# PSUM drains given to one engine each, a new issue order, and a last tile in two column halves

## The chip, the cores and the metric

The kernel runs on one core of a Trainium2 chip. The metric is the device time of one execution, in microseconds (us). "Span" is the time from the first to the last instruction in a profiled execution; in the runs here the measured time is 1.7 to 1.8 us longer. A transfer "lands" when its data has arrived; landing times are the issue time plus the time to landing. PSUM is the memory that matmuls write to, and from which ACT or DVE "drain" the result. The TensorE clock of the runs was 0.98 to 1.0. Runs of one kernel with 0.98 or 0.99 are up to 2 us longer than the others, so small differences are read from the profiled runs: in each of them the clock is 1.00 in every stretch up to 165 us. PE is TensorE, DVE VectorE, ACT ScalarE, POOL GpSimd and SP SyncE.

## The reference, cut to what matters

```python
# q, k, v: (8, 8, 576, 64)   phi: (8, 8, 576, 32)
a   = softmax(phi, axis=2)                    # over the sequence
k_m = einsum('bhsm,bhsd->bhmd', a, k)         # 32 memory slots per head
v_m = einsum('bhsm,bhsd->bhmd', a, v)
attn = softmax(q @ k_m.T / 8, axis=-1) @ v_m  # (8, 8, 576, 64)
x = attn.transpose(0, 2, 1, 3).reshape(8 * 576, 512)
h = maximum(maximum(x @ w1, x @ w2), x @ w3)  # 768 wide
out = h @ w_out                               # (4608, 512)
```

Nothing couples the eight batches except the weights. The kernel folds the small `v_m` of a batch into the weights (`v_m @ w`), so that the large matmuls run on the softmax result.

## The kernel before: the parts that matter

The kernel is a list of small pieces, issued in an order that is written out by hand. Each piece has a letter, a number, and a batch: `D2@3` is fold 2 of batch 3.

| letters | piece | who drains its PSUM tile |
|---|---|---|
| L0, L1, L2 | load phi; load k and v; load q | |
| E | exponential of phi (ACT) | |
| B, N, K | K/V product (72 matmuls), its normalisation (DVE), its transposes | DVE |
| Q0, Q1 | the two halves of q, transposed by DVE | |
| S | scores, two tiles | ACT (exponential) |
| M, R, X | sum, 1/sum (ACT, by logarithm), multiplication (DVE) | ACT |
| D0 to D3 | folds into the weights, 8 matmuls each | see `EVAC` |
| F0 to F11 | maxout pieces; even ones | ACT; odd ones DVE |
| T0 to T4 | output tiles of 128 rows; T4 takes 64 rows from each of two batches | see `EVAC` |
| Z*n* | *n* idle matmuls that keep PE busy while it waits for inputs | |

All matmul results go through one pool of four PSUM tiles, so a piece can start only when the fourth piece back has been drained:

```python
acc_pool = ctx.enter_context(
    tc.tile_pool(name="accp", bufs=4, space=bass.MemoryType.PSUM))
# ...
EVAC = {"D": "ssaa", "T": "aavaa"}

def evacuate(kind, n, out_, in_):
    e = EVAC[kind][n]
    if e == "s":                                   # shared
        nc.scalar.copy(out=out_[:, 0], in_=in_[:, 0])
        nc.vector.tensor_copy(out=out_[:, 1], in_=in_[:, 1])
    elif e == "a":
        nc.scalar.copy(out=out_, in_=in_)          # ACT
    else:
        nc.vector.tensor_copy(out=out_, in_=in_)   # DVE
```

Loads have two buffers per kind (phi, q; k and v together), so the load of batch b waits until batch b - 2 has been read. All but phi of the first batch are issued by POOL, in the order in which the L pieces stand. The end of the last output tile:

```python
h = [slice(0, DM // 2), slice(DM // 2, DM)]
nc.scalar.copy(out=ot[:, h[0]], in_=po[:, h[0]])
nc.vector.tensor_copy(out=ot[:, h[1]], in_=po[:, h[1]])
nc.scalar.dma_start(out=rows[:, h[0]], in_=ot[:, h[0]])
nc.sync.dma_start(out=rows[:, h[1]], in_=ot[:, h[1]])
```

The softmax here doesn't subtract the row's maximum and nothing guards it: scores larger than these inputs give would overflow.

## Time and profile before

| | before |
|---|---|
| time, median of the first 3 runs (lowest to highest) | 176.04 us (176.03 to 176.51) |
| span of the profiled run | 174.4 us |
| PE / ACT / DVE busy, share of the span | 93% / 62% / 58% |
| transfers saturated | until about 113 us |
| end of the last matmul; from there to the end of the span | 170.3 us; 4.1 us |

How to read it: PE is close to full, so the question is what its gaps are. A gap costs more than the idle time that the profile prints. The modelled end of a 512-column matmul lies 0.38 us after its start, but in a row they start every 0.215 us; the tail of 0.16 us is counted as busy though PE could already have worked on something else. So I compare starts with starts. The lines that carry the reading are in the prediction.

### The profile page before, as it was taken

To read this page: it belongs to the slowest core of one execution; us is meant where nothing else is said; L and a number is where in the kernel's file an instruction comes from. 1 tells how busy PE (TensorE), PEld (TensorE's weight loads), DVE (VectorE), ACT (ScalarE), POOL (GpSimd) and SP (SyncE) were. 2 spreads that over 40 slices of the span, in tenths; PEclk is the share of its full clock that TensorE was granted. 3 is DMA by queue.
4 is the path that set the end of the run, shared out by engine and by line. 5 is a ranking of instruction groups with operands and counts; after the bars stand their busy time and mean duration, and the time that the engine had idled before them with its cause. 6 is when DMAs were issued, how large, how long until landed. Compare 5 with 4: busy or idle time off the path is not lost.

```text
span 174.4 us, 4506 instructions
## 1 busy us (share of the span) xinstructions
PE 162.7 (93%) x1938; PEld 90.2 (52%) x1938; DVE 101.7 (58%) x160; ACT 108.3 (62%) x170; POOL 28.3 (16%) x43
## 2 busy tenths in 40 slices
PE   7989998998899999989999999999989998999990
PEld 2354543563377445746474564547645743476440
DVE  6408337787879188977577465673866535337010
ACT  4100367936986866988879587748864865652410
POOL 7951111132115102213203100000000000000000
PEclk9999999999999999999999999999999999999999
DMA  5999999999999999999999999712031112230333
GB/s 152 152 207 211 205 212 275 210 207 273 235 301 259 209 248 316 237 273 233 278 268 223 298 265 208 209 64 76 0 120 64 66 60 75 105 122 4 120 123 120
DMA packets 21973, 31.76 MB, mean 182 GB/s; under 512 B 1216, under 2 KB 16576, under 8 KB 21952
## 3 DMA queue, kind: packets, MB, share of 16 engines
q0 software_dynamic: 16080, 21.43, 64.0%
q1 hardware_dynamic: 5728, 9.90, 16.1%
q8 instruction: 15, 0.25, 0.5%
q10 hardware_dynamic: 144, 0.13, 0.2%
q14 instruction: 6, 0.05, 0.1%
HBM read 39.32 MB, written 9.44 MB: 280 GB/s over the span
## 4 chain that ended last, share of the span: by engine, by line
PE 70%; DVE 11%; ACT 10%; DMA 4%; issue 2%; POOL 0%; POOLq 0%
PE po L408 24%; PE acc L380 22%; PE po L417 7%; DVE wp L151 5%; PE po L140 5%; DMA kvo<-in_v_dram 4%; PE po L172 3%; ACT wp L150 2%; DVE qT L268 2%; PE kvp L216 2%; PE sm L311 2%; PE sc L290 2%; ACT ot L153 2%; ACT e L299 2%; ACT h L390 1%
## 5 line engine op out<-in xcount | busy, mean ns | idle before, releaser
L408 PE MATMUL po<-wo_sb,hT 128*128 128x512 bf16 x216 | 52.7, 379 | 1.8 <-DVE wp L151 1.5
L380 PE MATMUL acc<-attn,wp 128*128 128x288 bf16 x384 | 51.8, 286 | 0.6 <-DVE wp L151 0.5
L392 DVE TENSOR_TENSOR hT<-acc,h 128x576 bf16<-128x576 f32 x48 | 34.7, 751 | 23.0 <-PE acc L380 18.3
L380 PEld LDWEIGHTS <-wp 128*128 128x128 bf16 x384 | 36.6, 98 | 14.1 <-issue 2.0
L153 ACT COPY ot<-po 128x512 f32<-128x512 f32 x27 | 15.8, 585 | 30.6 <-PE po L417 25.5
L390 ACT ACTIVATE h<-acc 128x576 bf16<-128x576 f32 x48 | 29.3, 650 | 7.5 <-PE acc L380 7.5
L408 PEld LDWEIGHTS <-hT 128*128 128x128 bf16 x216 | 20.5, 97 | 24.7 <-issue 4.1
L268 DVE STREAM_TRANSPOSE qT<-qq 128x1152 bf16<-128x1152 bf16 x16 | 21.7, 1365 | 0.0
L299 ACT ACTIVATE e<-sc 128x576 bf16<-128x576 f32 x16 | 9.6, 654 | 16.0 <-PE sc L290 16.0
L417 PE MATMUL po<-wp,attn 128*128 128x512 bf16 x64 | 19.0, 379 | 0.0
L140 PE MATMUL po<-warm 128*128 128x512 bf16 x66 | 17.1, 412 | 1.2 <-DVE warm L128 1.2
L153 ACT CAST wp<-wps 128x1024 bf16<-128x1024 f32 x16 | 15.6, 1021 | 1.7 <-PE wps L355 1.6
L151 DVE CAST wp<-wps 128x512 bf16<-128x512 f32 x16 | 10.6, 686 | 9.1 <-ACT wp L150 9.1
L155 DVE COPY ot<-po 128x512 f32<-128x512 f32 x8 | 5.5, 690 | 17.6 <-PE po L417 17.6
L335 DVE TENSOR_TENSOR attn<-e,r 128x576 bf16<-128x576 bf16 x16 | 11.8, 746 | 2.6 <-ACT r L330 2.6
L104 POOL DMA_DIRECT2D qq<-in_q_dram x8 | 6.0, 746 | 34.8 <-DVE qT L268 18.3
L140 PEld LDWEIGHTS <-warm 128*128 128x128 bf16 x66 | 6.5, 104 | 9.3 <-issue 2.8
L330 ACT ACTIVATE r<-ln 128x576 f32<-128x576 f32 x16 | 10.9, 683 | 0.5
L205 ACT ACTIVATE e<-ph 128x1152 bf16<-128x1152 f32 (+1 forms) x9 | 9.5, 1054 | 1.7 <-DMA ph<-in_phi_dram 1.6
L324 ACT ACTIVATE ln<-sm 128x576 f32<-128x576 f32 x16 | 10.4, 648 | 0.0
L417 PEld LDWEIGHTS <-attn 128*128 128x128 bf16 x64 | 6.3, 98 | 7.4
L355 PE MATMUL wps<-w_sb,kvt 64*32 64x512 bf16 x192 | 8.2, 381 | 1.5 <-DVE wp L151 0.6
(43 smaller groups left out, 113.4 us busy)
## 6 DMA issues: line engine op xcount, KB each, us to landing
out_dram<-ot SPq DMA_DIRECT2D x35, 256.0 KB, 3.2
qq<-in_q_dram POOLq DMA_DIRECT2D x8, 576.0 KB, 17.2
ph<-in_phi_dram POOLq DMA_DIRECT2D x7, 576.0 KB, 18.0
kvo<-in_k_dram POOLq DMA_DIRECT2D x7, 576.0 KB, 19.1
kvo<-in_v_dram POOLq DMA_DIRECT2D x7, 576.0 KB, 21.2
w_sb<-in_moe_w_dram POOLq DMA_DIRECT2D x3, 768.0 KB, 19.3
wo_sb<-in_moe_w_out_dram POOLq DMA_DIRECT2D x1, 768.0 KB, 17.0
ph<-in_phi_dram SPq DMA_DIRECT2D x2, 288.0 KB, 3.0
```

What stands on the lines that cost most here:

```text
L140: nc.tensor.matmul(po[:, 0:BANK], lhsT=warm[:, 0:P], rhs=warm, start=True, stop=True)
L151: nc.vector.tensor_copy(out=out_[:, 1], in_=in_[:, 1])
L153: nc.scalar.copy(out=out_, in_=in_)
L268: nc.vector.transpose(out=s["qT"][:, j].rearrange("p j c h r -> p (j c h r)"), in_=loaded[b]["q"][:, j].rearrange("p j c d -> p (j c d)"),)
L299: nc.scalar.activation(out=e2[:, a].rearrange("p (t r c) -> p t r c", t=2, c=NC), in_=sc[a][:, :, 0:SH].rearrange("p t (c r) -> p t r c", ...
L330: nc.scalar.activation(out=r, in_=ln, func=AF.Exp, scale=-1.0)
L335: nc.vector.tensor_tensor(out=attns[b // 2][:, g, (b % 2) * S : (b % 2 + 1) * S], in0=s["e2"][:, g, 0:S], in1=s["r", g], op=ALU.mult,)
L380: nc.tensor.matmul(acc[:, h, 0:SH], lhsT=wps[b][:, g, w * DF + ft * P : w * DF + (ft + 1) * P], rhs=attn[:, g, c0 : c0 + SH], start=(g == ...
L390: nc.scalar.activation(out=h1, in_=a, func=AF.Relu)
L392: nc.vector.tensor_tensor(out=hT[:, ft, (b % 2) * S : (b % 2 + 1) * S].rearrange("p (h n) -> p h n", h=2), in0=a, in1=s["h1", ft], op=ALU.max,
L408: nc.tensor.matmul(po, lhsT=hT[:, fc, c0 : c0 + P], rhs=wo_sb[:, fc, :], start=(fc == 0), stop=False,)
L417: nc.tensor.matmul(po, lhsT=attn[:, g, c0 : c0 + P], rhs=wp3s[b][:, g, :], start=False, stop=(g == NG - 1),)
```

## The change

Its intent: no PSUM tile is drained by ACT and then DVE any more. All folds go to ACT, three of five kinds of output tiles to DVE. The order of all pieces is made anew for that. The last tile is computed in two column halves, each in a PSUM tile of its own, so that the first half is copied while the second is computed.

```diff
-    EVAC = {"D": "ssaa", "T": "aavaa"}
+    EVAC = {"D": "aaaa", "T": "avvva"}
 ...
+        if last:
+            return ffn2_last(b, c0)
 ...
+    def ffn2_last(b, c0):
+ ...
+        for i in range(2):
+            c = slice(i * DM // 2, (i + 1) * DM // 2)
+            po = acc_pool.tile([P, DM // 2], FP32, name="po", tag="acc")
+            # ... the same 8 matmuls, on wo_sb[:, fc, c] and wp3s[b][:, g, c]
+            rows = out[r0 : r0 + P, c]
+            if i == 0:
+                nc.vector.tensor_copy(out=ot[:, c], in_=po)
+                nc.sync.dma_start(out=rows, in_=ot[:, c])
+            else:
+                nc.scalar.copy(out=ot[:, c], in_=po)
+                nc.scalar.dma_start(out=rows, in_=ot[:, c])
 ... (the first 189 pieces of the list: all new)
     for b in range(4, B - 1):
-        run(b, "F0 F10 F1 F2 F8 S+ F9 F11 F6 L0+++++ F7 F4 Q1++ T4- M1+ R1+ E+++ F3 M0+")
-        run(b, "T2- F5 X1+ R0+ T3- D1+ D0+ B++ D2+ D3+ N++ T1 X0+ Q0++ L2++++ K++ L1++++")
-        run(b, "T0")
+        run(b, "T4- D3+ S+ L2++++ T3- F2 F4 Q1++ F5 F10 F3 F0 F6 F1 F8 M1+ F11 F9")
+        run(b, "L0+++++ F7 R1+ M0+ X1+ T2- R0+ D2+ B++ Q0++ D1+ N++ D0+ L1++++ T1 E+++")
+        run(b, "K++ X0+ T0")
-    run(B - 1, "T2- F4 F5 F10 F2 F6 T4- F11 F0 F8 F1 F3 F9 F7 T3- T3 T4 T2 T0")
-    ffn2(B - 1, 1, last=True)
+    run(B - 1, "F2 F10 F6 F3 F11 F0 T2- F1 F4 F8 F9 F7 F5 T3- T4 T4- T3 T2 T1")
+    ffn2(B - 1, 0, last=True)
```

(A `+` behind a piece means the next batch, `-` the one before.) The loads have new places too.

More of the change, by code (lines that the diff above doesn't have):

```diff
@@ L404, in ffn2 @@
         hT, attn = hts[b // 2], attns[b // 2]
+        c0 = S - HP if t == 4 else (b % 2) * (S + HP) + t * P
+        if last:
+            return ffn2_last(b, c0)
         po = acc_pool.tile([P, DM], FP32, name="po", tag="acc")
-        c0 = S - HP if t == 4 else (b % 2) * (S + HP) + t * P
         for fc in range(FT):
@@ L436, in ffn2 @@
         rows = out[r0 : r0 + P, :]
-        if not last:
-            evacuate("T", t, ot, po)
-            nc.sync.dma_start(out=rows, in_=ot)
-        else:
-            h = [slice(0, DM // 2), slice(DM // 2, DM)]
-            nc.scalar.copy(out=ot[:, h[0]], in_=po[:, h[0]])
-            nc.vector.tensor_copy(out=ot[:, h[1]], in_=po[:, h[1]])
-            nc.scalar.dma_start(out=rows[:, h[0]], in_=ot[:, h[0]])
-            nc.sync.dma_start(out=rows[:, h[1]], in_=ot[:, h[1]])
+        evacuate("T", t, ot, po)
+        nc.sync.dma_start(out=rows, in_=ot)
+    def ffn2_last(b, c0):
+        hT, attn = hts[b // 2], attns[b // 2]
+        ot = opool.tile([P, DM], FP32, name="ot")
+        r0 = (b // 2) * 2 * S + c0
+        for i in range(2):
+            c = slice(i * DM // 2, (i + 1) * DM // 2)
+            po = acc_pool.tile([P, DM // 2], FP32, name="po", tag="acc")
+            for fc in range(FT):
+                nc.tensor.matmul(
+                    po,
+                    lhsT=hT[:, fc, c0 : c0 + P],
+                    rhs=wo_sb[:, fc, c],
+                    start=(fc == 0),
+                    stop=False,
+                )
+            for g in range(NG):
+                nc.tensor.matmul(
+                    po,
+                    lhsT=attn[:, g, c0 : c0 + P],
+                    rhs=wp3s[b][:, g, c],
+                    start=False,
+                    stop=(g == NG - 1),
+                )
+            rows = out[r0 : r0 + P, c]
[5 more added lines that the diff above has]
+                nc.scalar.dma_start(out=rows, in_=ot[:, c])
     def first_kv():
@@ L484 @@
     for w in """
-        E@0 Z26@0 B@0 N@0 Z5@0 K@0 Q0@0 Q1@0 Z21@0 W0@0 L2@2 S@0 W1@0 L0@2 Z2@0 M0@0 R0@0
-        M1@0 W2@0 Z3@0 O0@0 X0@0 R1@0 L1@2 O3@0 X1@0 O2@0 O1@0 V0@0 D0@0 V1@0 D3@0 F2@0 V2@0
-        F0@0 D1@0 F4@0 D2@0 F6@0 F3@0 F1@0 E@1 F8@0 F10@0 F5@0 F7@0 F9@0 F11@0 B@1 N@1 T1@0
-        K@1 Q0@1 D2@1 D3@1 Q1@1 D1@1 T2@0 S@1 D0@1 M0@1 R0@1 M1@1 Q1@2 R1@1 T0@0 X0@1 X1@1
-        Q0@2 T3@0 F4@1 F0@1 F2@1 E@2 L0@3 L1@3 L2@3 F3@1 F1@1 F8@1 F5@1 B@2 N@2 F10@1 F11@1
-        F6@1 K@2 E@3 F9@1 F7@1 S@2 L2@4 L0@4 T1@1 L1@4 M0@2 M1@2 R1@2 T2@1 X1@2 R0@2 T0@1
-        X0@2 D1@2 D2@2 Q0@3 D0@2 B@3 T4@1 N@3 F6@2 F0@2 Q1@3 K@3 F4@2 F7@2 L0@5 S@3 F1@2
-        F10@2 Q0@4 F8@2 M1@3 F9@2 F11@2 R1@3 F2@2 F3@2 F5@2 E@4 M0@3 R0@3 X1@3 T3@1 D1@3
-        L2@5 D0@3 L1@5 L0@6 X0@3 B@4 N@4 D3@2 Q1@4 D2@3 T0@2 F0@3 F6@3 F1@3 F8@3 K@4 T2@2
-        L2@6 E@5 D3@4 D2@4 D3@3 Q0@5 L1@6 T1@2 F7@3 F4@3 F9@3 F5@3 F10@3 F2@3 F3@3 S@4 B@5
-        N@5 E@6 D1@4 D0@4 T3@2 L0@7 M0@4 L1@7 R0@4 M1@4 Q1@5 F11@3 R1@4 X0@4 T1@3 K@5 X1@4
-        L2@7 T0@3
+        E@0 Z26@0 B@0 N@0 Z5@0 K@0 Q0@0 Q1@0 Z15@0 S@0 Z6@0 M1@0 R1@0 W2@0 W0@0 W1@0 M0@0
+        X1@0 Z4@0 O0@0 O1@0 V0@0 R0@0 X0@0 O2@0 Z3@0 D0@0 V1@0 O3@0 F2@0 F6@0 V2@0 L2@2 F0@0
+        D1@0 F4@0 D2@0 F3@0 E@1 F1@0 F10@0 F7@0 L0@2 F11@0 F8@0 F9@0 F5@0 B@1 N@1 D3@0 K@1
+        D2@1 L1@2 D0@1 Q0@1 Q1@1 T1@0 D1@1 S@1 T3@0 M0@1 L0@3 Q0@2 M1@1 R0@1 R1@1 X0@1 X1@1
+        E@2 T0@0 T2@0 F8@1 Q1@2 F6@1 F7@1 F2@1 L2@3 F3@1 F9@1 F4@1 D3@1 B@2 F10@1 N@2 F5@1
+        F0@1 K@2 E@3 F1@1 F11@1 Q1@3 S@2 T0@1 Q0@3 M0@2 R0@2 X0@2 M1@2 L1@3 L0@4 T4@1 R1@2
+        L2@4 L1@4 T3@1 L0@5 X1@2 D0@2 D2@2 B@3 D1@2 N@3 T2@1 F2@2 K@3 F10@2 F3@2 F0@2 Q0@4
+        S@3 F11@2 F8@2 F4@2 F1@2 M1@3 F9@2 R1@3 E@4 F5@2 Q1@4 M0@3 R0@3 T1@1 F6@2 F7@2 D3@2
+        B@4 X1@3 D2@3 D0@3 T0@2 N@4 L0@6 X0@3 K@4 L2@5 F2@3 D1@3 S@4 T1@2 E@5 F3@3 F8@3 L1@5
+        F9@3 F6@3 F4@3 F10@3 L0@7 M1@4 F5@3 E@6 T2@2 R1@4 M0@4 F0@3 Q1@5 R0@4 F7@3 T3@2 L1@6
+        F1@3 L2@6 F11@3 D3@3 B@5 N@5 D0@4 D1@4 T0@3 X1@4 L1@7 K@5 T1@3 D3@4 Q0@5 D2@4 X0@4
+        L2@7
     """.split():
```

## The prediction

> **What bounds the kernel now.** I read, in this order: the page's busy shares and slices, the waits of TensorE, its timeline, the chain of waits, the groups of ACT and DVE by shape, and the landings of the input transfers.
>
> ```profile
> PE 162.7 (93%) x1938; PEld 90.2 (52%) x1938; DVE 101.7 (58%) x160; ACT 108.3 (62%) x170; POOL 28.3 (16%) x43
> ...
> DMA  5999999999999999999999999712031112230333
> ```
> TensorE (PE) is busy 93% of the 174.4 us span, ACT and DVE are far from full. But the DMA row is full for the first 26 of 40 slices, to about 113 us: the inputs arrive as fast as the transfers run. So there are two regimes, and I have to find where one hands over to the other.
>
> Where does PE wait for data? I add each transfer's time to landing to its issue time and compare with the step that reads it. The v input of batch 4 (issue from the timeline of POOL, landing from the DMA view):
>
> ```profile
> 54.52 0.75 POOL L96 DMA_DIRECT2D kvo<-in_v_dram  x1
> ```
> ```profile
> kvo<-in_v_dram POOLq DMA_DIRECT2D x1, 576.0 KB, 21.8
> ```
> ```profile
> 76.38 0.94 PE L216 MATMUL kvp<-kvo,e 64*32 64x192 bf16 x72 [0.51 <-ACT ot L153]
> ```
> 54.52 + 21.8 = 76.3, and the K/V product of batch 4 (step B@4) starts at 76.38. The row names an ACT copy as releaser, but that copy ended at 76.03; a normal hand-off here takes about 0.04 us, so I read this wait as one for the transfer. The same sum gives 37.2 for v of batch 1 (12.23 + 25.0), read at 37.38, and 52.0 for batch 2 (30.50 + 21.5), read at 52.52. Batch 5 lands at 87.8 and is read at 90.05; batch 6 lands at 100 and is read near 112. **So up to 76 us the transfers pace the kernel; after that PE and its waits do.**
>
> What PE waits for afterwards repeats once per batch. The timeline of PE in one round, then of ACT and DVE:
>
> ```profile
> 111.24 0.63 PE L355 MATMUL wps<-w_sb,kvt 64*32 64x512 bf16 x16
> 111.68 0.93 PE L216 MATMUL kvp<-kvo,e 64*32 64x192 bf16 x72
> 112.42 0.40 PE L355 MATMUL wps<-w_sb,kvt 64*32 64x512 bf16 x8
> 113.20 0.41 PE L355 MATMUL wps<-w3o,kvt 64*32 64x512 bf16 x8 [0.37 <-DVE wp L151]
> 113.80 0.38 PE L408 MATMUL po<-wo_sb,hT 128*128 128x512 bf16 x1 [0.19 <-DVE wp L151]
> ```
> ```profile
> 111.83 1.08 ACT L150 CAST wp<-wps 128x512 bf16<-128x512 f32 x2
> 112.89 1.93 ACT L153 CAST wp<-wps 128x1024 bf16<-128x1024 f32 x2
> ```
> ```profile
> 112.45 1.29 DVE L151 CAST wp<-wps 128x512 bf16<-128x512 f32 x2 [1.30 <-ACT wp L150]
> ```
> Four folds (8 matmuls each, 0.22 us) stand almost together, each needs one of four PSUM buffers, and the drains are slower. The shared drain (ACT one half, DVE the other) does not run in parallel: DVE starts only after ACT. PE loses more than the printed idle: from 112.42, 0.22 us of work should let the next fold start at 112.64, it starts at 113.20, so 0.56 is lost; then 113.42 to 113.80, 0.38.
>
> The end of the kernel, from the timeline:
>
> ```profile
> 170.31 0.37 ACT L442 COPY ot<-po 128x256 f32<-128x256 f32 x1 [1.14 <-PE po L417]
> 170.71 0.37 ACTq L444 DMA_DIRECT2D out_dram<-ot  x1
> 170.71 0.42 DVE L443 COPY ot<-po 128x256 f32<-128x256 f32 x1 [3.17 <-ACT ot L442]
> 171.16 0.33 SPq L445 DMA_DIRECT2D out_dram<-ot  x1
> ```
> PE ends at 170.3, the span at 174.4. The halves of the last tile are also copied one after the other.
>
> **What the Trainium skill says.** (1) "PSUM — Partial Sum Buffer", section "PSUM bank collisions raise a hardware error": two engines must not touch the same bank and quadrant at once, two reads included, and the answer is to guard by bank. The last tile is one 512-column bank, so its two copies must be serial, and the trace shows it (DVE from 170.71). The fold's halves are in different banks, which the page calls harmless, yet this kernel orders them too (1.30 us wait). (2) "TensorE: Matmul & The Clock Gate", section "Back-to-back issue gap": about N/2.4 + 2.5 ns per matmul, when warm. The trace agrees: six 512-column matmuls step in 1.29 us, 0.215 each; twenty of 288 in 2.45, 0.1225. For 256 columns this estimates 0.109. (3) "Perfetto Trace Analysis", section "Optimizing Scalar/DVE Operations": each ACT or DVE operation has a fixed overhead, so one large is cheaper than two small. Here: ACT 128x1024 is 1.02 us, two 128x512 are 1.20. (4) "DMA: Bandwidth & Descriptors", section "Anatomy of one DMA": the fixed part, about 2 us, is mostly completion. The last two 128 KB stores take 1.7 and 1.8 us to landing; the change keeps them.
>
> **The change, part by part.**
>
> ```profile
> L153 ACT COPY ot<-po 128x512 f32<-128x512 f32 x27 | 15.8, 585 | 30.6 <-PE po L417 25.5
> L153 ACT CAST wp<-wps 128x1024 bf16<-128x1024 f32 x16 | 15.6, 1021 | 1.7 <-PE wps L355 1.6
> L151 DVE CAST wp<-wps 128x512 bf16<-128x512 f32 x16 | 10.6, 686 | 9.1 <-ACT wp L150 9.1
> L155 DVE COPY ot<-po 128x512 f32<-128x512 f32 x8 | 5.5, 690 | 17.6 <-PE po L417 17.6
> ```
> *Drains.* Sixteen shared fold drains (0.60 on ACT, then 0.69 on DVE, so 1.29 until the buffer is free) become ACT drains of 1.02. To pay for it, output tiles 1 and 3 go to DVE beside tile 2. Per batch ACT gains 2 x (1.02 - 0.60) = +0.84 and loses 2 x 0.585 = -1.17 of tile copies; DVE loses 2 x 0.686 = -1.37 and gains 2 x 0.690 = +1.38. Totals barely move (ACT -0.3, DVE 0 per batch). What moves is latency, 0.27 per fold, and DVE no longer stands idle behind ACT.
>
> *Order.* From the order of instructions: in the loop the folds no longer stand together. Fold 3 goes to the start of a round ahead of the scores, and folds 2, 1, 0 have the K/V product and then a 1.73 us tile behind them. Walking one round by hand with the durations above and four buffers, each drain ends at or before its buffer is needed; I find at most 0.1 to 0.3 us of waiting per round, against 0.56 + 0.38 = 0.94 now. The warm-up fillers are 68 instead of 66, but lie ahead of the 37 us pin. The loads of batches 2 to 4 are the same set ahead of v of batch 4, so B@4 stays pinned near 76.4.
>
> *Sum from B@4 on.* Before: 170.3 - 76.4 = 93.9 us. Pure work left: 24 tiles x 1.73, 3 split tiles x 1.94, 60 maxout pieces x 0.49, 19 folds x 0.22, 4 K/V products x 0.77, 4 scores x 0.40, 8 sums x 0.245, 4 transposes x 0.17 = 88.2. Of the excess 5.7, the PE timeline shows some 4.6 as waits: 0.33 (77.6), 0.19 and 0.21 (84.2, 91.3), 0.63 (sums at 93.2), 0.37 (96.2), 1.87 (two rounds of 0.94), 0.99 (147.5). The other 1.1 are small restarts after changes of shape, which stay. After: one more fold is left (88.4), plus 1.1, plus new waits. For batch 3, where the order is uneven, my walk gives 0.65 (ACT is nearly full: two exponentials of phi and two logs there), and for the loop 0.6. So 76.4 + 88.4 + 1.1 + 1.3 = 167.2, against 170.3: **-3.1**.
>
> *Last tile.* Two halves of 8 matmuls of 256 columns: 16 x 0.109 = 1.75 against 8 x 0.215 = 1.73, nothing. The first half is drained beside the second's matmuls; after the last matmul only one 0.37 copy and a store stand. The DVE copy of 0.42 and its hand-off go: **-0.4**, so 3.7 after PE's end in place of 4.1.
>
> Span 167.2 + 3.7 = 170.9. The measured time exceeds the span by some 1.7 (176.04 against 174.4, 176.16 in the profiled run): **172.6 us**, a ratio of 0.980.
>
> **Rivals.** (a) *The transfers pace more than I think.* In the new order q of batch 3 is loaded ahead of its k and v, and phi of batch 6 ahead of batch 5. Then v of batch 3 lands near 64.0 instead of 60.6 and its product, now at 63.08, would slip about 1 us; later ones have 2 us of slack at batch 5. If that slip reaches B@4, the time is 173.5 to 174.5. For it: DMA is full. Against it: after it only 11.7 us of work stand before B@4, so 64.0 + 11.7 still meets 76.4. (b) *ACT becomes the bound.* Its load per batch is about 14.0 us in a 16.7 us round, and all folds queue there in order behind logs and exponentials; if each loop round loses 0.8 as now, only the tail is saved: 175 to 175.5. Against: the load falls by 0.3 and the folds are spread. (c) *The early waits count too.* Some 3 us of PE waits lie between 37 and 76; if the pins are softer than I read, removing them gives 171 or less. Against: 76.3 to 76.4 agree too well.
>
> **Range and chances.** All waits gone: about 171.3. Rival (a) or half of (b): 174.3. The 2% line is 172.5, practically at my centre; hand walks miss waits more often than they invent them, so I lean slightly to "within". Slower needs a transfer to starve, which nothing suggests.
>
> **What will show it.** B@4 should start within 0.5 us of 76.4 and v of batch 4 land just before it. No wait on DVE's half of wp can remain, and idle of PE in the rounds from 98 to 150 should shrink to a third. PE should end near 167.2, the span 3.7 later. Wrong if B@4 moves by over 1 us, if waits on ACT's wp replace those on DVE, or if the tail keeps its 4.1.

## The result, and the profile after

| | before | after |
|---|---|---|
| time, median of 4 runs (lowest to highest) | 176.03 us (175.97 to 176.51) | 173.66 us (173.47 to 174.53) |
| ratio of the fast runs | | 0.9869 (95%: 0.9832 to 0.9906) |
| span of the profiled run | 174.4 | 171.7 |
| K/V product of batch 4 starts | 76.38 | 76.18 |
| last matmul ends | 170.3 | 168.0 |
| from there to the end of the span | 4.1 | 3.7 |

The change makes the kernel 1.3% faster. Ratios here and below are the mean time of one kernel's fast runs over that of the other's fast runs in the same rounds, so they are not quite the ratio of the medians that are quoted.

The repeating loss at the folds is gone. The timeline of PE after the change, at the place that answers to 111.24 to 113.80 before, and then ACT there:

```profile
111.64 0.41 PE L355 MATMUL wps<-w_sb,kvt 64*32 64x512 bf16 x8
111.86 0.93 PE L216 MATMUL kvp<-kvo,e 64*32 64x192 bf16 x72
112.61 0.62 PE L355 MATMUL wps<-w_sb,kvt 64*32 64x512 bf16 x16
113.18 1.46 PE L410 MATMUL po<-wo_sb,hT 128*128 128x512 bf16 x5
```
```profile
112.12 2.88 ACT L153 CAST wp<-wps 128x1024 bf16<-128x1024 f32 x3 [0.74 <-PE wps L355]
```

No idle stands before any of the four. ACT still takes 2.88 us for three folds, but the next 1.73 us tile (L410) needs a buffer that is already free, and so runs beside the drains. The end of the kernel:

```profile
167.17 0.42 DVE L468 COPY ot<-po 128x256 f32<-128x256 f32 x1 [0.18 <-PE po L459]
167.63 0.33 SPq L469 DMA_DIRECT2D out_dram<-ot  x1
167.63 0.38 PE L459 MATMUL po<-wp,attn 128*128 128x256 bf16 x2
168.05 0.37 ACT L471 COPY ot<-po 128x256 f32<-128x256 f32 x1 [6.44 <-PE po L459]
```

The first half's copy (DVE, 167.17) lies beside the second half's matmuls; one copy follows the last matmul.

But a wait has appeared that was not there before. PE and DVE in the first round of the loop, and the transfer that DVE names (its issue, and its time to landing):

```profile
102.31 3.10 PE L380 MATMUL acc<-attn,wp 128*128 128x288 bf16 x24
106.39 1.63 PE L380 MATMUL acc<-attn,wp 128*128 128x288 bf16 x12 [0.97 <-DVE hT L392]
```
```profile
104.32 1.38 DVE L268 STREAM_TRANSPOSE qT<-qq 128x1152 bf16<-128x1152 bf16 x1 [1.11 <-DMA qq<-in_q_dram]
```
```profile
86.55 0.75 POOL L104 DMA_DIRECT2D qq<-in_q_dram  x1
```
```profile
qq<-in_q_dram POOLq DMA_DIRECT2D x1, 576.0 KB, 17.7
```

86.55 + 17.7 = 104.25: q of batch 6 lands, and 0.07 us later DVE begins to transpose it (Q1@6). While it stood there, the odd maxout pieces behind it in DVE's order were not drained, and PE ran out of buffers. The same sum in the trace of before gives a landing at 93.4, 11 us earlier.

The busy times of all engines in the loop rounds, before and after (columns: window, its length, then PE, PEld, DVE, ACT, POOL busy, clock, share of the transfer engines, GB/s):

```profile
98.00:150.00 52.00, 50.07 (x611) 28.92 (x610) 30.59 (x48) 36.88 (x59) 0.00 (x0) 1.00 0.43 120
```
```profile
98.00:150.00 52.00, 50.59 (x609) 29.53 (x616) 32.40 (x50) 38.79 (x56) 0.74 (x1) 1.00 0.49 123
```

PE's idle time goes from 1.93 to 1.41 us, and 0.97 of what is left is that one wait.

### The profile page after: what moved, and what is told of

It is laid out like the page before. It is cut to its first block, busy times and chain, and to the rows that moved or that the text cites. A ratio compares the mean times of both kernels' runs of the same rounds, so it can differ in the third digit from the quotient of the medians.

```text
span 171.7 us, 4491 instructions
## 1 busy us (share of the span) xinstructions
PE 161.2 (94%) x1925; PEld 91.5 (53%) x1948; DVE 102.4 (60%) x160; ACT 107.5 (63%) x154; POOL 28.3 (17%) x43
## 4 chain that ended last, share of the span: by engine, by line
PE 43%; DMA 41%; issue 6%; DVE 3%; POOL 3%; ACT 1%; POOLq 0%
DMA kvo<-in_v_dram 20%; PE po L410 16%; PE acc L380 15%; DMA ph<-in_phi_dram 11%; DMA qq<-in_q_dram 10%; PE po L419 5%; POOL kvo L96 3%; PE wps L355 2%; PE kvp L216 2%; DVE qT L268 2%; PE sm L311 1%; PE po L451 1%; PE po L428 1%; ACT e L205 1%; PE sc L290 0%
## 5 line engine op out<-in xcount | busy, mean ns | idle before, releaser
L380 PE MATMUL acc<-attn,wp 128*128 128x288 bf16 x384 | 51.2, 286 | 1.3 <-DVE hT L392 1.0
L410 PE MATMUL po<-wo_sb,hT 128*128 128x512 bf16 x191 | 50.1, 379 | 1.1
L153 ACT CAST wp<-wps 128x1024 bf16<-128x1024 f32 x32 | 31.3, 1017 | 10.3 <-PE wps L355 10.2
L155 DVE COPY ot<-po 128x512 f32<-128x512 f32 x24 | 16.6, 690 | 30.5 <-PE po L419 30.5
L410 PEld LDWEIGHTS <-hT 128*128 128x128 bf16 x210 | 19.4, 98 | 23.2 <-issue 4.4
L140 PE MATMUL po<-warm 128*128 128x512 bf16 x65 | 18.2, 428 | 1.5 <-DVE warm L128 1.2
L419 PE MATMUL po<-wp,attn 128*128 128x512 bf16 x62 | 18.4, 379 | 0.0
L153 ACT COPY ot<-po 128x512 f32<-128x512 f32 x11 | 6.4, 584 | 11.4 <-PE po L428 6.3
L89 POOL DMA_DIRECT2D ph<-in_phi_dram x7 | 5.3, 756 | 36.9 <-ACT e L205 33.4
L216 PE MATMUL kvp<-kvo,e 64*32 64x192 bf16 x576 | 8.3, 243 | 0.8 <-DMA kvo<-in_v_dram 0.8
```

What stands on the lines that cost most here:

```text
L140: nc.tensor.matmul(po[:, 0:BANK], lhsT=warm[:, 0:P], rhs=warm, start=True, stop=True)
L216: nc.tensor.matmul(kvp[M * j : M * (j + 1), a, 0 : 3 * D], lhsT=s["e"][r, j, c, :], rhs=kv[r, :, j, c, :], start=(c == 0), stop=(c == NC - 1),
L380: nc.tensor.matmul(acc[:, h, 0:SH], lhsT=wps[b][:, g, w * DF + ft * P : w * DF + (ft + 1) * P], rhs=attn[:, g, c0 : c0 + SH], start=(g == ...
L410: nc.tensor.matmul(po, lhsT=hT[:, fc, c0 : c0 + P], rhs=wo_sb[:, fc, :], start=(fc == 0), stop=False,)
L419: nc.tensor.matmul(po, lhsT=attn[:, g, c0 : c0 + P], rhs=wp3s[b][:, g, :], start=False, stop=(g == NG - 1),)
```

## The experiments

After the result I held this theory: the drains and the order remove the waits at the folds, the split tile saves 0.4 us at the end, and part of the gain is given back to late transfers, most of it at q of batch 6. The rivals: one part of the change does it all; the transfers pace both kernels alike; PE's work alone bounds, and the landing is a coincidence. Each experiment's ratio is to the kernel before, run on the same chip.

### Drains and order apart

Two kernels fill the table that the change jumps across. The first is before with `EVAC` of the change; the second is the change with `EVAC` of before:

```diff
 old_order_new_drains:  -    EVAC = {"D": "ssaa", "T": "aavaa"}
                        +    EVAC = {"D": "aaaa", "T": "avvva"}
 new_order_old_drains:  the reverse, in the changed kernel
```

> The order of before, the drains of the change. Main theory: what costs before is the slow shared drain (1.29 us until the buffer is free, now 1.02) where folds stand together; ACT then does four drains of 1.02 in a row, so PE still waits for ACT at 113 us: the 0.94 us lost there per round falls by about 0.3 (D3 waits for D0's drain 0.27 earlier, T for D1's 0.27 x 2). Together some 1 us less after 76 us: 174.5 to 175.3. Rival (the order alone carries the gain): within 0.4 of before, 175.6 to 176.4. Rival (drains alone carry it): 174 or less.

> The order of the change, the shared drains of before. Main theory: in the new order folds are spread, so a drain of 1.29 in place of 1.02 is mostly hidden, but DVE now stands behind ACT for its half and has tiles 1 and 3 no longer: 174 to 175, some 0.5 to 1 us above the change. Rival (only the drains count): back to 175.5 or more.

| time, ratio to before | old drains | new drains |
|---|---|---|
| old order | 1 | 175.74 us, 0.9952 (0.9925 to 0.9979) |
| new order (split tile) | 178.07 us, 1.0102 (1.0052 to 1.0151) | 173.66 us, 0.9869 |

The new drains alone gain 0.5%, some 0.85 us by the ratio, where 0.7 to 1.5 were expected (the time itself would also fit the first rival). But in the round that I had worked out they gain less than I wrote. The ACT and PE timelines of that run:

```profile
112.40 3.76 ACT L153 CAST wp<-wps 128x1024 bf16<-128x1024 f32 x4 [1.24 <-PE wps L355]
```
```profile
113.46 0.41 PE L355 MATMUL wps<-w3o,kvt 64*32 64x512 bf16 x8
114.38 1.46 PE L408 MATMUL po<-wo_sb,hT 128*128 128x512 bf16 x6 [0.50 <-ACT wp L153]
```

Four drains stand in one row on ACT. PE loses 114.38 - 113.46 - 0.22 = 0.70 us here and 0.14 at the fold ahead, together 0.84 against 0.94 before. The wait has changed its name from DVE to ACT and has hardly shrunk: where the folds stand together, two engines in turn or one engine four times is nearly the same.

The second kernel was a miss: I expected 174 to 175 us, and it is slower than before. DVE and PE early in that run, then the same DVE step in the change:

```profile
42.11 0.69 DVE L151 CAST wp<-wps 128x512 bf16<-128x512 f32 x1 [2.07 <-ACT wp L150]
42.71 2.63 DVE L268 STREAM_TRANSPOSE qT<-qq 128x1152 bf16<-128x1152 bf16 x2
```
```profile
44.14 0.31 PE L290 MATMUL sc<-qT,kvt 32*32 32x288 bf16 x8 [1.25 <-DVE qT L268]
45.40 0.44 PE L290 MATMUL sc<-qT,kvt 32*32 32x288 bf16 x24 [0.94 <-DVE qT L268]
```
```profile
40.23 2.64 DVE L268 STREAM_TRANSPOSE qT<-qq 128x1152 bf16<-128x1152 bf16 x2
```

DVE keeps the order of its list. Its half of a shared drain now stands ahead of the transposes of q; it waits 2.07 us for ACT's half, and the transposes, whose data is there, start 2.5 us later (42.71 against 40.23). PE waits 2.2 us for the scores. From K/V product 1 to product 2 it takes 17.92 us (37.28 to 55.20), against 15.47 in the change (37.50 to 52.97): this place makes 2.4 of the 4.0 us between the two profiled runs; the 1.6 us lost behind product 4 were not taken apart. So the cost of a shared drain is not only its own 1.29 us: it makes everything behind it on DVE wait for ACT. My expectation had counted DVE's load and not the blocking. **Order and drains are one change**: alone, one gives 0.5% and the other loses 1.0%; together they give 1.2% (0.9885, the change without its split tile, below).

### The last tile alone

In one kernel the last tile of before is split as in the change, in the other the changed kernel has the last tile of before.

```diff
 before_split_tail:  + ffn2_last(...) and its call, otherwise before
 after_whole_tail:   - ffn2_last(...); the last copies as in before, otherwise the change
```

> Before, only the last tile in two column halves. Theory: the second copy (DVE 0.42 us and hand-off) leaves the end: 0.4 to 0.45 us less, 175.6. Rival (the last store waits on something else): no change.

> The change, but with the last tile as before. Theory: 0.4 to 0.45 us more than the change, about 174.1. Rival: the same as the change, 173.66.

Measured: 175.73 us, 0.9965 (0.994 to 0.999), and 174.29 us, 0.9885 (0.986 to 0.991). Both have the expected sign, but the times alone do not tell the second from the change (0.9869). The profile is sharper: from the end of the last matmul to the end of the span it is 4.1 us in before and in `after_whole_tail`, but 3.7 in the change and in `before_split_tail`. The split is worth 0.4 us, whatever stands ahead of it.

### Do the transfers pace the kernel until 76 us?

The prediction says that before is paced by transfers until the K/V product of batch 4 at 76.4 us, and that PE waits ahead of it are free. If so, PE work added ahead of it costs nothing, and smaller loads save something.

```diff
 before_fill_mid:  -  ... F2@2 F3@2 F5@2 E@4 ...
                   +  ... F2@2 F3@2 F5@2 Z3@0 E@4 ...      # 3 idle matmuls, 0.65 us
 before_half_kv:   -  for h in halves if b == 0 else [slice(0, NP)]:
                   +  for h in halves if b == 0 else [slice(0, NP if b == 1 else NP // 2)]:
```

> Before, with 0.65 us of idle matmuls (three of 512 columns) put in ahead of K/V product 4, near 73 us. Theory (that product waits for v of batch 4, landing at 76.3, and PE has 0.7 us to spare ahead of it): 0 to 0.2 us more than before. Rival (PE itself is the bound there, or the ACT copy that the profile names): 0.65 more, 176.7.

> Before, but from batch 2 on only half of k and v is loaded (wrong result on purpose), so every input lands earlier. After the filler run my view is: in before the waits on the shared drains bound, transfers cost little: 175.3 to 176.2. My first view (transfers pace before until 76 us, a pin that hides some 3 us of PE waits): the waits there stay, since they are waits for drains, but B@4 starts some 0.7 us earlier and 175 to 175.6 comes out. If transfers paced it fully: 173 or less.

Measured: 177.04 us, 1.005 (1.0033 to 1.0067), with the filler: it shows in full. With half of k and v (its result is wrong): 176.42 us, 1.0007 (0.9973 to 1.0041): nothing is gained. My theory of before falls. The half-load run shows why, in the timeline of PE:

```profile
75.83 0.63 PE L355 MATMUL wps<-w_sb,kvt 64*32 64x512 bf16 x16
76.28 0.93 PE L216 MATMUL kvp<-kvo,e 64*32 64x192 bf16 x72
...
77.89 0.41 PE L355 MATMUL wps<-w_sb,kvt 64*32 64x512 bf16 x8 [0.47 <-DVE wp L151]
78.48 1.46 PE L408 MATMUL po<-wo_sb,hT 128*128 128x512 bf16 x5 [0.19 <-DVE wp L151]
```

With v there in time, the product follows the two folds at once (75.83 to 76.28). So I had read the wait at 76.38 rightly: it was for the transfer. But the tile that comes next (L408) does not start any earlier. From the output tile ahead of the folds to this one it takes 78.48 - 74.02 = 4.46 us; in before it is 77.89 - 73.42 = 4.47. The time saved ahead of the product comes back as a wait for the shared drains (0.47), which had run on in before while PE stood waiting for v. Two waits lay side by side, and the one that the transfer caused ended first. The profiled runs differ by up to 1.2 us in the start of K/V product 1 (37.0 to 38.2), also between kernels with the same pieces ahead of it. Counted from there to the end of the last matmul, before takes 132.9 us, with half of k and v 132.9, with the filler 133.5.

### And in the change?

```diff
 after_fill_mid:   -  ... E@4 F5@2 Q1@4 ...
                   +  ... E@4 F5@2 Z3@0 Q1@4 ...
 after_fill_late:  -  ... F5 T3- T4 T4- T3 T2 T1
                   +  ... F5 T3- T4 T4- Z3 T3 T2 T1
 after_half_kv:    as before_half_kv, in the changed kernel
```

> The change with the same 0.65 us of idle matmuls near 73 us. Theory (the next thing that holds the change is q of batch 6 landing at 104.25, with 1.1 us lost there): the filler is absorbed, 0 to 0.3 us more than the change. Rival (PE work bounds everywhere): 0.65 more, 174.3.

> Control: the change with the same filler among the last tiles, near 161 us, where every theory says that PE alone bounds: 0.65 more than the change, 174.3.

> The change, with half of k and v from batch 2 on (wrong result on purpose). Theory (the change has run into the transfers: q of batch 6 costs 1.1 us, q of batch 4 some 0.6 us): both waits go, 171.8 to 172.4, so more gain than in before. Rival (transfers are equal for both): the same gain as in before.

| | time | ratio to before |
|---|---|---|
| the change | 173.66 us | 0.9869 (0.9832 to 0.9906) |
| with 0.65 us of filler near 73 us | 173.25 | 0.9839 (0.9819 to 0.986) |
| with 0.65 us of filler near 161 us | 174.51 | 0.9902 (0.9878 to 0.9927) |
| with half of k and v | 171.3 | 0.9717 (0.9694 to 0.974) |

The filler at 73 us costs nothing. The same filler at 161 us costs 0.33% of 176, some 0.6 us; against the change that is within the noise, but its runs (173.79 to 175.04) and those of the filler at 73 us (173.03 to 173.73) do not overlap, so the control works. Smaller loads (wrong result again) save 1.5%, more than expected, where they saved nothing in before. Counted from K/V product 1 to the end of the last matmul, they save 1.8 us (128.7 against 130.5): 0.7 ahead of product 4, where DVE waits for q of batch 4 in the change, and 1.1 behind it. So **the change has turned a kernel that waited for drains into one that waits for transfers.** One table ties it together, from the profiled runs of the four kernels with the loads of the change in which PE stands at this place (in `new_order_old_drains` PE comes later and does not wait there; `after_q_read_later`, below, moves the reader):

| | q of batch 6 lands | PE goes on at | last matmul ends | landing to end |
|---|---|---|---|---|
| the change | 104.25 | 106.39 | 168.01 | 63.8 |
| filler near 73 us | 103.87 | 105.96 | 167.58 | 63.7 |
| whole last tile | 104.71 | 106.83 | 168.43 | 63.7 |
| filler near 161 us | 104.81 | 106.88 | 169.14 | 64.3, less 0.65 of filler: 63.7 |

When the transfer lands, the end is fixed to a tenth of a microsecond. The run with the filler at 73 us is even a little quicker than the change, as its transfer happened to land 0.38 us earlier.

### Mending it

If the landing is the cause, q of batch 6 loaded earlier must remove the loss; so must reading it later.

```diff
 after_q_first:       -  ... L0@6 X0@3 K@4 L2@5 ... F10@3 L0@7 M1@4 ... L1@6 F1@3 L2@6 ...
                      +  ... L2@5 X0@3 K@4 L0@6 ... F10@3 L2@6 M1@4 ... L1@6 F1@3 L0@7 ...
 after_q_read_later:  -  F2 F4 Q1++ F5 F10 F3 F0 F6 F1 F8 ...
                      +  F2 F4 F5 F10 F3 F0 F6 F1 Q1++ F8 ...
 after_q_first_2:     after_q_first, and
                      -  ... L1@3 L0@4 T4@1 R1@2 L2@4 ...   B@4 X1@3 D2@3 D0@3 T0@2
                      +  ... L1@3 L2@4 T4@1 R1@2 L0@4 ...   D2@3 D0@3 B@4 X1@3 T0@2
```

> The change, but q of batch 5 is loaded ahead of phi of batch 6, and q of batch 6 ahead of phi, k, v of its turn. Main theory: in the change DVE stands 1.11 us until q of batch 6 lands (104.25) and PE loses some 1.1 us at 105.4 to 106.4; loaded first, q lands near 94 and this goes: 172.4 to 172.7, PE ends near 166.9. Rival (PE's wait is for ACT or a buffer, the landing is a coincidence): 173.4 to 173.9. Rival 2 (the wait moves to v of batch 5 or 6): between.

> The change with its own load order, but in the loop DVE's transpose of the second half of q (Q1 of the batch after next) stands behind six maxout pieces more, some 2.5 us later. Theory (the loss comes from a DVE instruction that waits for a late transfer and holds up the maxout drains behind it): q of batch 6 has landed by then or nearly, the 1 us wait of PE goes, 172.4 to 172.9, about as with q loaded first. Rival (the total of transfers holds the kernel, wherever q is read): as the change, 173.5 to 173.8. Rival 2 (DVE's order is so tight that any move costs elsewhere in the three rounds): 173.5 or more, with new waits of PE on DVE in the later rounds.

> The mended load order (q of batches 5 and 6 first), and also q of batch 4 ahead of phi of batch 4, and folds 2 and 0 of batch 3 ahead of K/V product 4. Theory: DVE's 0.72 us wait for q of batch 4 and PE's 0.63 at 71.5 go, and the folds keep PE busy until v of batch 4 lands near 76: 0.4 to 0.5 us less than with the first mend, 172.0. Rival (that wait was hidden by v of batch 4, landing at 76): as with the first mend, 172.5.

*q first*: 172.51 us, 0.981 (0.9775 to 0.9844), as expected. q of batch 6 lands at 92.2, and the 36 maxout matmuls run through, as its PE timeline shows (102.31 to 106.39 and on in the change):

```profile
102.17 4.57 PE L380 MATMUL acc<-attn,wp 128*128 128x288 bf16 x36
106.58 0.41 PE L311 MATMUL sm<-e,blkones 128*128 128x288 bf16 x2
```

From the K/V product of batch 4 to the last matmul's end it takes 90.69 us, against 91.83 in the change: the 1.14 us between them is what the wait had cost. With half of k and v it is 90.71, so behind that product q of batch 6 was all that the transfers cost; the other 1.0 us of the half-load run is gained ahead of it (75.03 against 76.03).

*q read later*: 173.86 us, 0.9845 (0.9803 to 0.9888), not told apart from the change. The wait for the transfer is gone, but the second rival of the expectation came true. In the PE timeline:

```profile
109.66 1.46 PE L410 MATMUL po<-wo_sb,hT 128*128 128x512 bf16 x5 [0.39 <-DVE hT L392]
...
126.14 1.46 PE L410 MATMUL po<-wo_sb,hT 128*128 128x512 bf16 x5 [0.40 <-DVE hT L392]
```

The transpose of 1.37 us now stands ahead of the last drains of each round, and an output tile waits for its buffer. From the product of batch 4 to the end it is 91.82 us, as in the change: one wait of 1.1 us was traded for two of about half.

*q of batch 4 first too*: median of the five fast runs 172.51 us, 0.9809 (0.9764 to 0.9855; a sixth was slow and is left out). The times don't tell it from *q first*, and with this interval they could not tell a gain of 0.4 us. Its wait of PE at 71.5 us went, but PE then waited 0.38 us for a buffer at 76.57 (v had landed at 75.93, so this wait is not the rival's), and the tile behind it started at 77.44 instead of 77.38. But in this run K/V product 1 had started 0.41 us later (37.57 against 37.16). Counted from there, the tile comes 0.35 us sooner and the last matmul ends after 129.2 us instead of 129.6. So one run's profile speaks for most of the expected gain, and whether it is real stays open.

The best version that I found is therefore the change with q of batches 5 and 6 loaded first, 1.9% faster than before (with q of batch 4 first too, it is not told apart).

## Why the prediction was right or wrong

**The time and the range: right.** 173.66 us lies between the 171.3 ("all waits gone") and the 174.3 (a rival come true) that its text names as ends, 1.1 us above the centre. It leaned to "within 2%", and that came.

**The end of the kernel: right.** 3.7 us after the last matmul were predicted and measured; the split costs PE nothing (six 256-column matmuls step in 0.65 us).

**The waits at the folds: right in the mechanism.** DVE has no half to drain any more, and no such wait is left. In the rounds from 98 to 150 us PE's idle time without the new wait is 0.44 us of 1.93, less than the third that I foretold; with it, it is 1.41, so this sign did not come as written. The latency term, "0.27 per fold", was not what did it: the new drains in the old order changed the round by 0.10 us. The spread of the folds did, together with DVE being freed from standing behind ACT.

**The sum from the product of batch 4 on: its last term was mis-sized.** It was 88.4 of work, 1.1 of restarts and 1.3 of new waits, 90.8 in all; measured, 91.83. The term "for the loop 0.6" is the one: the loop loses 1.14 to q of batch 6 alone. Without it 90.69 is measured, the sum to a tenth.

**Rival (a) had the right kind of cause and the wrong place.** It looked for transfers that come late by the new load order, and named q of batch 3 and phi of batch 6. I missed the third reordering, q of batch 6 from first to last of its group. Those two cost nothing that shows.

**"Up to 76 us the transfers pace the kernel": wrong for before.** The product does wait for v, as read. But product 2, which I had counted as a second hit (52.0 and 52.52), was no wait: 28 matmuls of 288 columns started at 48.99 and at 0.1225 each fill PE to 52.42. What failed above all is the step to "earlier waits are free": the filler cost before 0.5%, and smaller loads gave it nothing, because the drains of the folds ended later than that wait. Rival (c), "the early waits count too", was right about before. The product of batch 4 starts at 76.18 in the change, where I foretold 76.4, but by a coincidence: PE reaches it there 0.12 us after v has landed (76.06), with no idle ahead of it.

Why did removing the early drain waits not bring that product forward more? The work between products 1 and 4 is the same in both orders (35.0 us by the durations of the prediction), and it takes 38.68 us in the change against 39.00 in before. Of the waits that the new order brings in their place, 0.7 us is the one by q of batch 4 that half of k and v removes. The larger one is not for a transfer. The new order puts the transposes of batch 1 (K) behind its product with only one fold between them, as the PE timeline of the change shows:

```profile
39.06 0.23 PE L256 MATMUL kvtp<-ident,kvn 128*128 128x128 bf16 x1 [0.41 <-DVE kvn L232]
39.58 0.28 PE L256 MATMUL kvtp<-ident,kvn 128*128 128x128 bf16 x2 [0.29 <-DVE kvn L240]
40.31 0.63 PE L355 MATMUL wps<-w_sb,kvt 64*32 64x512 bf16 x16 [0.45 <-DVE kvt L258]
```

From the end of that fold's work (38.24 + 0.22) to 40.31 there is 0.17 us of work, so 1.68 us are lost in waits for DVE's normalisation and copy. In before, with an output tile between them, 0.62 us is lost there. The prediction did not look at this place, since it took all waits ahead of product 4 for free. No run moved these transposes back, so what that would give is not shown.

## What to carry to other kernels

A step that waits for a transfer need not be on the path: ask what else is under way during that wait, and when it ends; a filler of known length ahead of the step, and a control filler where one engine surely bounds, answer it in two runs. An instruction on an in-order engine that waits for another engine, or for a late transfer, costs what stands behind it, so such instructions are placed by what follows them. And after a new issue order, check the landing of every transfer against its first reader: here one load moved to the end of its group took back 1.1 us of a gain of 3.8 (176.3 to 172.5).

## What the Trainium skill lacked or had wrong

- "TensorE: Matmul & The Clock Gate", section "Back-to-back issue gap", says that in a stream of weight load and matmul pairs 512 columns take about 131 ns each and 128 columns about 81, and that its formula N/2.4 + 2.5 ns, which it gives for an isolated matmul, is too high for large N. The prediction used that formula for matmuls in a row without saying so. Here the formula held in streams of such pairs at three sizes: 0.215 us for 512, 0.1225 for 288, 0.108 for 256 (six in 0.65 us).
- "DMA: Bandwidth & Descriptors", section "Anatomy of one DMA", gives a time for one transfer issued by GpSimd, as the loads here are: about 2 us and the bytes over 436 GB/s. For the 576 KB loads here that would be an estimated 3.4 us; in the full queue they took 4 to 26 us to landing, and what decided was the place in the issue order (q of batch 6: 92.2 or 104.25 us with the same bytes). The page does not say how to plan a queue that is always full.
- No page that I read says what an in-order engine loses behind a wait that depends on another engine: here a 0.69 us copy that waited 2.07 us for ACT put two transposes off by 2.5 us.
